# Moving small VectorE steps between the groups of a fused attention and gated feed-forward kernel

## The chip, the cores and the metric

The kernel runs on one core of a Trainium2 chip. A core has five engines that run their own streams of instructions and wait for each other by semaphores: PE (TensorE, matmuls), DVE (VectorE), ACT (ScalarE), POOL (GpSimd) and SP (SyncE, which here only issues DMAs). The metric is the device time of one execution in microseconds (us); less is better.

## What is computed

The reference, cut to its core: a linear attention without softmax, an RMS norm per head, and a gated feed-forward layer over all tokens.

```python
# q, k, v: (8 batches, 8 heads, 576 tokens, 64)
kv  = einsum('bhsd,bhse->bhde', k, v)
out = einsum('bhsd,bhde->bhse', q, kv)
x   = out / sqrt(mean(out * out, axis=-1) + 1e-6) * g_norm   # then (4608, 512)
g, val = x @ w_gate, x @ w_val                               # (4608, 1536)
gelu = 0.5 * g * (1 + erf(g / sqrt(2)))
ffn_out = gelu * val @ w_out
result = x + sigmoid(x @ w_res) * ffn_out
```

## The kernel before

**Blocks.** Each of the 8 batches gives a block of 512 tokens, as four rows of tiles (j = 0 to 3, 128 tokens by 512 columns). The 64 tokens of each batch that are left over, the "last tokens", are gathered two batches to a row into a ninth block, number 8. The attention of batch b is worked out while TensorE does the feed-forward of blocks b-2 and b-1: `a_o` multiplies q by kv, `a_sq` and `a_red` make the sums of squares `ss`, `a_norm` makes the reciprocal roots `ny` (on POOL from batch 2 on), `a_t` scales the attention's output by them into the tile `t` (L341, VectorE), `a_x` multiplies a row of `t` by g in place (L355, VectorE), and `d_xT` transposes rows of `t` into `xT` with a DMA on SP's queue. For batches 4 to 7 `a_t(b, 4)` scales the last tokens; its source is not a PSUM bank but the SBUF tile `o32`, one of three buffers that it shares with the tiles `c` named below.

**A block's two stages.** In the first, the gate and value products, TensorE multiplies `xT` by `w_gate` and `w_val`. For the last third of block 0 and from the fifth column tile of block 2 on, this is done in groups of four column tiles (`gv_group`), with seven products in place of eight, of sums of weights and of tokens (`ts`). Block 2 has two such groups, blocks 3 to 8 have three. Each group is a list of words, written out by hand; for groups that are not the last of a block it reads

```python
"1g 1v Eg 5g Ev 5v dg 6g dv 6v Fg 2g Fv 2v 7g g11 7v cg 3g cv 3v h11 g12 4g g21 h12 4v g22 h21 h22"
```

A number is a product on TensorE (four matmuls, L736) for the gate (g) or the value (v): 1, 4, 6, 7 add to a PSUM bank A, 2 to E, 3 and 5 to F. E and d are copies on ScalarE (bank A to E, L746; F to the SBUF tile d, L750). F and c are sums on VectorE (L757): F puts A + d back into bank F, c puts A + d into an SBUF tile `c`. g11 to g22 are gelus on ScalarE (L767), h11 to h21 products with the value on VectorE, and h22 the same on POOL (L773). A product that adds to a bank waits until those who read the bank before are done: 6 for E, 7 for F, 4 for c.

In the second stage (`out_by_products`) come the residual gate (`m_res`), then seven products with `w_out` in banks named wA to wF, `s_rest` (VectorE sums of hidden tiles), the multiplication with the gate `pf` (L527), the addition of `t` on POOL (`fin`, L531), and `store`, a DMA on SP's queue. The calls of `aside` put VectorE and POOL steps of the coming block between the products. For block 1 alone (`later`) the steps `a_x`, `fin` and `store` are put into block 2's groups, since its `t` is multiplied by g only then.

**What sets the order.** Every engine executes its instructions in the order in which this program issues them. `at_word(block, i, word, *steps)` issues steps directly behind a word in the i-th group of a block; `at` and `aside_out` do so behind a slot and inside the second stage. The steps that are moved:

- block 1's rows in block 2: `a_x(1, 0..3)` (x0 to x3), four `fin`, two `store`; L570 to L573;
- in blocks 3 to 6 (`whole(m + 1)`), for the batch that follows, b = 4 to 7: `a_t(b, 2)` to `a_t(b, 4)` (t2, t3, t4), `a_x(b, 0..4)` (x0 to x4), two `d_xT`; L1220 to L1231.

At the end of block 2's last group stands `load_behind` (L1134), with which POOL issues the loads of the next batch; behind it POOL does `a_norm`.

Of the kernel before, what the change touches and what calls it, by code (L numbers as in the profile page):

```python
# [18 lines left out]
def kernel(  # L19
# [22 lines left out]
    NJ = 4  # L42
# [284 lines left out]
    def where(b, j):  # L327
        return (b, j) if j < NJ else (B, pair(b))
# [40 lines left out]
    def d_xT(b, j0, j1):  # L369
        blk, k0 = where(b, j0)  # L370
        k1 = k0 + j1 - j0
        nc.sync.dma_start(
            out=xT_t[blk][:, k0:k1, :, :].rearrange("p j c t -> p (j c) t"),
            in_=t_t[blk][:, k0:k1, :].rearrange("p j c -> p (j c)"),
            transpose=True,
        )
# [35 lines left out]
    def m_res(blk, j, bank):  # L412
        rps = pmoe.tile([P, C], FP32, name="rps", bank=bank)
        for cc in range(NP):
            nc.tensor.matmul(  # L415
                rps,
                lhsT=xT_t[blk][:, j, cc, :],
                rhs=wr16[:, cc, :],
                start=(cc == 0),
                stop=(cc == NP - 1),  # L420
            )

        th = th_all[:, j, :]
        nc.scalar.activation(out=th, in_=rps, func=AF.Tanh, scale=0.5)  # L424
        return th
# [30 lines left out]
    def b_of(i, j):  # L456
        return wo16[:, (i - 1) * NFH : i * NFH, (j - 1) * CH : j * CH]

    def a_of(blk, i, j):
        return hids[blk][:, (j - 1) * NFH : j * NFH, (i - 1) * PR : i * PR]  # L460
# [20 lines left out]
    def s_last(blk):  # L481
        sub(nc.vector, hid_sums[3], a_of(blk, 1, 2), hid_sums[1])
# [14 lines left out]
    def out_by_products(blk, later, banks, amid):  # L497
        w = {}
        s_ = hid_sums

        def aside(ahead_of):
            for f in amid.get(ahead_of, ()):
                f()

        def res(jj):
            for j in (2 * jj, 2 * jj + 1):
                m_res(blk, j, banks[j])

        def first_two():
            for n in ("D", "E", "F", "A"):  # L510
                w[n] = pmoe.tile([P, 2, CH], FP32, name="w" + n, bank=banks[n])
            w["d"] = attnp.tile([P, 2, CH], FP32, tag="sq", bufs=3, name="wd")
            s_last(blk)
            prod(w["A"], a_of(blk, 1, 1), b_of(1, 1), True)
            nc.scalar.copy(out=w["E"], in_=w["A"])
            aside("D")
            prod(w["D"], s_[0], wo_t[:, 0], True)
            nc.scalar.copy(out=w["d"], in_=w["D"])
            aside("gates")
            for j in range(NJ):  # L520
                m_sigmoid(j)

        def part(jj):
            return slice(None), slice(2 * jj[0], 2 * jj[0] + 2), slice(jj[1] * CH, (jj[1] + 1) * CH)

        def pf(jj, src, eng=nc.vector):
            eng.tensor_tensor(out=res_all[part(jj)], in0=th_all[part(jj)], in1=src, op=ALU.mult)  # L527

        def fin(jj):
            of = part(jj)  # L530
            nc.gpsimd.tensor_tensor(out=res_all[of], in0=res_all[of], in1=t_t[blk][of], op=ALU.add)  # L531

        def store(jj):
            dst = out[blk * S : blk * S + M0, :].rearrange("(p j) c -> p j c", j=NJ)
            js = slice(2 * jj, 2 * jj + 2)
            nc.sync.dma_start(out=dst[:, js, :], in_=res_all[:, js, :])

        def others():


            prod(w["A"], s_[1], wo_t[:, 1], False)
            aside("F")
            sub(nc.vector, w["F"], w["A"], w["d"], ALU.add)
            aside("00")
            prod(w["E"], a_of(blk, 1, 2), b_of(2, 1), False)
            pf((0, 0), w["E"])
            aside("22")
            prod(w["A"], s_[2], wo_t[:, 2], False)
            c22 = res_all[part((1, 1))]
            sub(nc.vector, c22, w["A"], w["d"], ALU.add)  # L550
            aside("01")
            prod(w["F"], s_[3], b_of(2, 2), False)
            pf((0, 1), w["F"])
            aside("11")
            prod(w["A"], a_of(blk, 2, 2), wo_t[:, 3], False)
            if whole(blk + 1):
                pf((1, 1), c22, nc.gpsimd)
                pf((1, 0), w["A"])
            else:
                pf((1, 1), c22)  # L560
                pf((1, 0), w["A"])
            if later:
                return
            for i in (1, 0):
                fin((i, i))
                fin((i, 1 - i))
                store(i)

        if later:
            x = [lambda j=j: a_x(blk, j) for j in range(NJ)]  # L570
            at_word(blk + 1, 0, "Fv", x[0])
            at_word(blk + 1, 0, "h21", *x[1:3], lambda: fin((0, 0)), lambda: fin((0, 1)), lambda: store(0))
            at_word(blk + 1, 1, "Fv", x[3], lambda: fin((1, 0)), lambda: fin((1, 1)), lambda: store(1))  # L573
        return [lambda: res(0), lambda: res(1), first_two, others]

    def out_last(blk, banks):
# [243 lines left out]
    for which in "kv":  # L820
        if which == "k":
            t = hidp.tile([P, NF, NJ * P], FP16, tag="hid", name=which + "f").rearrange("p a b -> p (a b)")
        else:
            t = hid_s
# [8 lines left out]
    for which in "kv":  # L833
        t = hid_of[which]
# [336 lines left out]
    def at_word(blk, i, word, *fs):  # L1171
        amid_gv.setdefault((blk, i), {}).setdefault(word, []).extend(fs)
# [5 lines left out]
    def plan_attn_ahead(b):  # L1178

        rem = pair(b) is not None  # L1180
        m = b - 2
        assert rem == (m in GROUPS)
        act, pool = nc.scalar.copy, nc.gpsimd
        begin = [lambda: attn_begin(b), lambda: d_qT(b)]
        if rem:
            begin.append(lambda: d_rem_qT(b))
        if m in GROUPS:
            for i in range(2):
                half = lambda i=i: by_token(b, act, slice(2 * i, 2 * i + 2))
                if whole(m):  # L1190
                    at_word(m, i, "g11", half)
                else:
                    at(m, 2 + i, half)
            if whole(m):
                at_word(m, 1, "g11", *begin)
            else:
                at(m, 3, *begin)
            if b + 1 < B:
                at(m, 2 * GF, lambda: load_behind(b))
            last = len(GROUPS[m]) - 1  # L1200
        else:
            at(m, 8, lambda: by_token(b, act, slice(0, 2)))
            at(m, 9, lambda: by_token(b, act, slice(2, 4)), *begin)
            at(m, NF - 1, lambda: a_kv(b, act))
            at(m, NF, lambda: load_behind(b))
        if rem:
            own = 2 * pair(b) + 1 == b
            at_word(m, last, "5v" if own else "3v", lambda: a_rem_kv(b))
            at_word(m, last, "dv" if own else "g12", lambda: kv_out(b))
            at_word(m, last, "h21", *[lambda: rem_mm(b)] * own, lambda: rem_out(b), lambda: a_sq(b, NJ))  # L1210
        at(m, NF, lambda: a_o(b), *[lambda: a_red(b, NJ)] * rem, lambda: a_ss(b, 0), lambda: a_ss(b, 1))
        aside_out(m, "D", lambda: a_ss(b, 2), lambda: a_ss(b, 3))
        aside_out(m, "F", lambda: a_norm(b, 0, NJ + rem, pool))
        first = [lambda: new_block(b), lambda: a_t(b, 0), lambda: a_t(b, 1)]
        if whole(m + 1):
            aside_out(m, "11", *first)
        else:
            at(m, NF + 3, *first)
        if whole(m + 1):
            t = [lambda j=j: a_t(b, j) for j in range(NJ + 1)]  # L1220
            x = [lambda j=j: a_x(b, j) for j in range(NJ + 1)]
            for i, word, fs in (
                (0, "Fv", t[2:3]),
                (0, "cv", t[3:4]),
                (0, "h21", t[4:5]),
                (1, "1v", x[0:1]),
                (1, "Fv", x[1:2]),
                (1, "cv", x[2:3]),
                (2, "1v", [x[3], lambda: d_xT(b, 0, NJ), x[4], lambda: d_xT(b, NJ, NJ + 1)]),
            ):  # L1230
                at_word(m + 1, i, word, *fs)  # L1231
            return
        for j in range(2, NJ + rem):
            at(m + 1, j - 2, lambda j=j: a_t(b, j))
        for j in range(NJ):
            at(m + 1, 2 + j // 2, lambda j=j: a_x(b, j))
        at(m + 1, 3, lambda: d_xT(b, 0, NJ))
        if rem:
            at_word(m + 1, 0, "h21", lambda: a_x(b, NJ), lambda: d_xT(b, NJ, NJ + 1))
# [13 lines left out]
    for blk in GROUPS:  # L1253
        t = token_sums(blk, nc.vector)
# [160 lines left out]
```

## Time and profile before

| | |
|---|---|
| median of 4 runs | 325.11 us (324.84 to 326.05) |
| the profiled execution | 325.38 us, of which the span from first to last instruction 323.5 us |
| granted TensorE clock, mean | 0.995 |
| PE busy | 315.7 us, 98% of the span |
| DVE busy | 264.7 us, 82% |
| ACT busy | 201.5 us, 62% |
| POOL busy | 145.9 us, 45% |

All are of one profiled execution but the first. A busy share is time with at least one instruction in work; PE's matmuls are pipelined and their ends are modelled, so that a PE that is busy all the time may still have its steps start late.

The stages that the change touches, in us from the span's start, with the busy time in each:

| stretch | stage | PE | DVE | ACT | POOL |
|---|---|---|---|---|---|
| 98.1 to 104.2 | block 2, first group | 6.10 | 5.22 | 4.25 | 0.00 |
| 104.2 to 111.4 | block 2, last group | 7.20 | 6.51 | 5.16 | 5.66 |
| 111.4 to 124.7 | block 2, second stage | 13.30 | 11.77 | 8.81 | 12.25 |
| 124.7 to 131.2 | block 3, first group | 6.43 | 5.31 | 4.52 | 5.58 |
| 131.2 to 137.6 | block 3, second group | 6.40 | 6.40 | 5.25 | 1.16 |
| 137.6 to 144.9 | block 3, third group | 7.30 | 7.11 | 5.13 | 2.88 |

Blocks 4 to 6 repeat block 3's pattern every 33.2 us.

### The profile page before, as it was taken

The page shows a single profiled execution, that of the slowest core. Times are in us where ns is not written, and L with a number is a line of the kernel's source. Part 1 is how long each engine was busy: PE and PEld are TensorE (multiplying, and loading weights), DVE is VectorE, ACT ScalarE, POOL GpSimd, SP SyncE. Part 2 cuts the span into 40 slices and gives each one's busy share as a digit, 9 for nine tenths or more (in the row PEclk, how much of TensorE's full clock was granted, in tenths as well). Part 3 has the DMA queues.
Part 4 walks back from the last instruction along what each step waited for, and adds up shares of the span by engine and source line. Part 5 has one row for each costly group of instructions (what it writes and reads, how often), then busy time and mean ns, then how long its engine had stood idle before and what let it go on. Part 6 is the DMA issues. An engine that isn't in the chain of part 4 may idle for free.

```text
span 323.5 us, 7457 instructions
## 1 busy us (share of the span) xinstructions
PE 315.7 (98%) x2936; PEld 236.9 (73%) x2936; DVE 264.7 (82%) x482; ACT 201.5 (62%) x367; POOL 145.9 (45%) x212
## 2 busy tenths in 40 slices
PE   8999999999999999999999999999999999999993
PEld 3544755445858778887888688868887888788782
DVE  5788879799798897998799879898996777677754
ACT  3673685365737783778486848684766467636760
POOL 2792351573700999247833784117511242042232
PEclk9999999999999999999999999999999999999998
DMA  7999999799995489299938893820321030002004
GB/s 252 325 203 204 194 205 180 167 178 136 153 138 107 141 134 146 114 161 131 98 132 164 110 120 131 127 41 2 130 50 33 2 130 4 0 30 104 0 2 130
DMA packets 76693, 38.89 MB, mean 120 GB/s; under 512 B 42098, under 2 KB 74354, under 8 KB 76658
## 3 DMA queue, kind: packets, MB, share of 16 engines
q0 software_dynamic: 38752, 17.17, 42.4%
q1 hardware_dynamic: 37328, 20.71, 24.6%
q8 instruction: 23, 0.38, 0.5%
q10 hardware_dynamic: 578, 0.52, 0.5%
q14 instruction: 12, 0.10, 0.1%
HBM read 38.80 MB, written 9.44 MB: 149 GB/s over the span
## 4 chain that ended last, share of the span: by engine, by line
PE 96%; DVE 3%; ACT 0%; issue 0%; DVEq 0%; ACTq 0%
PE Av L736 12%; PE Ag L736 11%; PE wA L488 11%; PE rps L415 10%; PE gps L395 6%; PE vps L395 6%; PE Fg L736 6%; PE Fv L736 6%; PE fps L432 3%; PE Ev L736 3%; PE Eg L736 3%; PE wE L488 3%; PE wD L488 3%; PE wF L488 3%; PE w L488 2%; PE idle L901 2%
## 5 line engine op out<-in xcount | busy, mean ns | idle before, releaser
L773 POOL TENSOR_TENSOR hid<-ge,c 128x512 f16<-128x512 f16 x21 | 25.4, 1207 | 65.0 <-ACT ge L767 65.0
L531 POOL TENSOR_TENSOR osb<-osb,t 128x512 f32<-128x512 f32 x28 | 31.7, 1164 | 41.3 <-DVE osb L527 25.2
L488 PEld LDWEIGHTS <-hid_s 128*128 128x128 f16 x384 | 37.6, 98 | 4.3
L736 PEld LDWEIGHTS <-wsv 128*128 128x128 f16 x336 | 32.8, 98 | 5.1 <-issue 0.9
L736 PEld LDWEIGHTS <-wsg 128*128 128x128 f16 x336 | 32.7, 98 | 4.4
L415 PE MATMUL rps<-wr,xT 128*128 128x512 f16 x144 | 33.4, 380 | 0.0
L488 PEld LDWEIGHTS <-hid 128*128 128x128 f16 x288 | 28.2, 98 | 5.0
L746 ACT COPY Eg<-Ag 128x512 f32<-128x512 f32 x21 | 12.2, 583 | 25.9 <-PE Ag L736 25.9
L757 DVE TENSOR_TENSOR Fg<-Ag,d 128x512 f32<-128x512 f32 x21 | 14.6, 695 | 15.8 <-ACT d L750 10.9
L383 ACT ACTIVATE ge<-gps 128x512 f16<-128x512 f32 x24 | 14.1, 597 | 21.3 <-PE gps L395 21.1
L736 PEld LDWEIGHTS <-wg 128*128 128x128 f16 x252 | 24.4, 98 | 3.3
L736 PEld LDWEIGHTS <-wv 128*128 128x128 f16 x252 | 24.6, 98 | 3.0
L424 ACT ACTIVATE th<-rps 128x512 f32<-128x512 f32 x36 | 21.1, 595 | 8.0 <-PE rps L415 8.0
L736 PE MATMUL Av<-ts,wsv 128*128 128x256 f16 x168 | 25.2, 272 | 0.1
L736 PE MATMUL Ag<-ts,wsg 128*128 128x256 f16 x168 | 25.2, 272 | 0.0
L254 DVE TENSOR_REDUCE ss<-sq 128x8 f32<-128x512 f32 x32 | 20.1, 678 | 4.7 <-ACT sq L249 4.6
L415 PEld LDWEIGHTS <-xT 128*128 128x128 f16 x144 | 13.5, 98 | 14.2
L395 PE MATMUL gps<-xT,wg 128*128 128x512 f16 x88 | 22.6, 379 | 0.0
L395 PE MATMUL vps<-xT,wv 128*128 128x512 f16 x88 | 22.6, 379 | 0.0
L488 PE MATMUL wA<-wo_ts,hid_s 128*128 128x256 f16 x168 | 20.6, 273 | 0.0
L384 DVE TENSOR_TENSOR hid<-ge,vps 128x512 f16<-128x512 f16 x24 | 16.3, 684 | 4.8 <-PE vps L395 4.0
L429 ACT ACTIVATE th<-th 128x512 f32<-128x512 f32 x36 | 20.1, 642 | 0.0
(188 smaller groups left out, 766.8 us busy)
## 6 DMA issues: line engine op xcount, KB each, us to landing
out_dram<-osb SPq DMA_DIRECT2D x14, 512.0 KB, 2.6
qraw<-in_q_dram POOLq DMA_DIRECT2D x7, 512.0 KB, 6.9
k<-in_k_dram POOLq DMA_DIRECT2D x7, 512.0 KB, 9.6
v<-in_v_dram POOLq DMA_DIRECT2D x7, 512.0 KB, 11.6
wg<-in_moe_w_gate_dram POOLq DMA_DIRECT2D x2, 512.0 KB, 8.2
wv<-in_moe_w_val_dram POOLq DMA_DIRECT2D x2, 512.0 KB, 8.9
wo<-in_moe_w_out_dram POOLq DMA_DIRECT2D x2, 512.0 KB, 13.6
out_dram<-osb SPq DMA_DIRECT2D x4, 256.0 KB, 4.5
```

Of the source, the lines that this page charges most:

```text
L254: nc.vector.tensor_reduce(out=out_, in_=sqs.pop((b, i)), op=ALU.add, axis=mybir.AxisListType.X)
L383: nc.scalar.activation(out=ge, in_=gps, func=AF.Gelu)
L384: nc.vector.tensor_tensor(out=hids[blk][:, f, :], in0=ge, in1=vps, op=ALU.mult)
L395: nc.tensor.matmul(ps[:, j0 * P : j1 * P], lhsT=w[:, cc, :], rhs=xT_t[blk][:, j0:j1, cc, :], start=(cc == 0 and j0 == 0), stop=(cc == NP - ...
L415: nc.tensor.matmul(rps, lhsT=xT_t[blk][:, j, cc, :], rhs=wr16[:, cc, :], start=(cc == 0), stop=(cc == NP - 1),)
L424: nc.scalar.activation(out=th, in_=rps, func=AF.Tanh, scale=0.5)
L429: nc.scalar.activation(out=th, in_=th, func=AF.Copy, scale=0.5, bias=0.5)
L488: nc.tensor.matmul(ps[:, e - es[0], :], lhsT=a[:, f, e * P : (e + 1) * P], rhs=b[:, f, :], start=(start and e == es[0] and f == 0), stop=( ...
L531: nc.gpsimd.tensor_tensor(out=res_all[of], in0=res_all[of], in1=t_t[blk][of], op=ALU.add)
L736: nc.tensor.matmul(out_[:, r, :], lhsT=lhsT, rhs=rhs, start=(first and r == 0 and c == 0), stop=(c == 1), skip_group_check=True,)
L757: nc.vector.tensor_tensor(out=dst, in0=ps["A", u], in1=sb["d", u], op=ALU.add)
L773: eng.tensor_tensor(out=dst, in0=ge[q], in1=source(q, "v"), op=ALU.mult)
```

## The change

It moves steps between words and leaves all arithmetic as it is.

```diff
@@ out_by_products, block 1's rows in block 2
             x = [lambda j=j: a_x(blk, j) for j in range(NJ)]
-            at_word(blk + 1, 0, "Fv", x[0])
-            at_word(blk + 1, 0, "h21", *x[1:3], lambda: fin((0, 0)), lambda: fin((0, 1)), lambda: store(0))
-            at_word(blk + 1, 1, "Fv", x[3], lambda: fin((1, 0)), lambda: fin((1, 1)), lambda: store(1))
+            at_word(blk + 1, 0, "1v", *x[0:2], lambda: fin((0, 0)), lambda: fin((0, 1)), lambda: store(0))
+            at_word(blk + 1, 0, "Fv", x[2])
+            at_word(blk + 1, 0, "cv", x[3])
+            at_word(blk + 1, 0, "h22", lambda: fin((1, 0)), lambda: fin((1, 1)), lambda: store(1))
@@ plan_attn_ahead, batches 4 to 7 in blocks 3 to 6
                 (0, "Fv", t[2:3]),
                 (0, "cv", t[3:4]),
-                (0, "h21", t[4:5]),
                 (1, "1v", x[0:1]),
-                (1, "Fv", x[1:2]),
-                (1, "cv", x[2:3]),
-                (2, "1v", [x[3], lambda: d_xT(b, 0, NJ), x[4], lambda: d_xT(b, NJ, NJ + 1)]),
+                (1, "Fv", t[4:5]),
+                (1, "cv", x[1:2]),
+                (2, "1v", [*x[2:4], lambda: d_xT(b, 0, NJ)]),
+                (2, "Fv", [x[4], lambda: d_xT(b, NJ, NJ + 1)]),
```

So t4 goes from the end of the first group into the second, behind Fv; x1 goes from Fv to cv of the second group, x2 from there into the third, x4 from the third group's start behind its Fv. In block 2 all four products with g and all four `fin` are issued in the first group, two of each at its start.

## The prediction

> **What bounds the kernel now.** I read the page's chain of waits first: it is TensorE nearly alone.
>
> ```profile
> PE 96%; DVE 3%; ACT 0%; issue 0%; DVEq 0%; ACTq 0%
> ```
>
> So only what makes TensorE stand still counts, and a busy share hides that, since matmuls overlap. I therefore read the timeline of TensorE by the starts of its steps. In a group (L736) a step is four matmuls, and undisturbed steps start 0.437 us apart; a longer distance is a stall. I took all distances from block 2 to the end. Block 2 has none over 0.44, blocks 7 and 8 none either. In blocks 3 to 6 the second group always has two. Block 3:
>
> ```profile
> 133.84 0.60 PE L736 MATMUL Eg<-xT,wg 128*128 128x256 f16 x4
> 134.28 0.60 PE L736 MATMUL Ev<-xT,wv 128*128 128x256 f16 x4
> 134.85 0.60 PE L736 MATMUL Ag<-ts,wsg 128*128 128x256 f16 x4
> 135.44 0.60 PE L736 MATMUL Av<-ts,wsv 128*128 128x256 f16 x4
> 135.88 0.60 PE L736 MATMUL Fg<-xT,wsg 128*128 128x256 f16 x4
> ```
>
> The columns are start, duration, engine. 134.28 to 134.85 is 0.57 (0.13 lost), 134.85 to 135.44 is 0.59 (0.155 lost). In blocks 4, 5, 6 the same two lose 0.29, 0.285, 0.295. These are words 7g and 7v: they add to bank A, so they wait until VectorE has read A in Fg and Fv. VectorE there:
>
> ```profile
> 133.04 0.81 DVE L341 TENSOR_TENSOR t<-o,ny 128x512 f16<-128x512 f32 x1
> 133.77 0.41 DVE L355 TENSOR_TENSOR t<-t,g 128x512 f16<-128x512 f16 x1
> 134.11 0.69 DVE L757 TENSOR_TENSOR Fg<-Ag,d 128x512 f32<-128x512 f32 x1
> 134.71 0.68 DVE L757 TENSOR_TENSOR Fv<-Av,d 128x512 f32<-128x512 f32 x1
> 135.31 0.41 DVE L355 TENSOR_TENSOR t<-t,g 128x512 f16<-128x512 f16 x1
> 135.64 0.68 DVE L757 TENSOR_TENSOR c<-Ag,d 128x512 f32<-128x512 f32 x1
> 136.24 0.68 DVE L757 TENSOR_TENSOR c<-Av,d 128x512 f32<-128x512 f32 x1
> ```
>
> Fg ends at 134.79 and 7g starts 0.06 later; Fv ends at 135.39, 7v starts 0.05 later. In front of Fg stand the scaling of the last tokens (t4, 0.73 to the next start) and a product with g (0.34). The copies d that Fg and Fv need end on ScalarE at 133.69 and 134.17, so they are not the bound.
>
> **Edit 1, t4 from h21 of the first group to Fv of the second (blocks 3 to 6).** The product x0 now starts at 133.04. A POOL product (hid, L773) runs until 133.30; a product with g that meets one is held to its end and ends 0.28 later:
>
> ```profile
> 138.58 1.16 POOL L773 TENSOR_TENSOR hid<-ge,c 128x512 f16<-128x512 f16 x1 [5.28 <-ACT ge L767]
> 138.96 1.06 DVE L355 TENSOR_TENSOR t<-t,g 128x512 f16<-128x512 f16 x1
> ```
>
> So x0 ends at 133.59, before d: free. Fg then starts with d, at 133.75 (VectorE starts 0.03 to 0.09 after a ScalarE copy), ends 134.44; Fv 134.35 to 135.03. Undisturbed, 7g is due at 134.72 and 7v at 135.16: both stalls go. What is late next: t4 (0.68 without POOL beside it, like t2; step 0.60) runs 134.95 to 135.63, cg 135.55 to 136.24, cv 136.15 to 136.83. 4g (due 136.47) is free; 4v (due 136.90) needs cv plus 0.055, so within 0.02. The first group, which has t2 at the same word, loses 0.04 there. I take 0.03 lost against 0.29 gained. Bounds for t4: 0.60 as t2, or 0.73 as it was; with 0.73 cv ends 0.13 later and 4v loses 0.12. It had the POOL product until 133.30 beside it, so I take 0.60. cg also now writes the o32 buffer that t4 has just read; a step that must wait for its predecessor on VectorE (the second ts of L463) starts 0.03 after its end instead of 0.08 before, so at worst 0.11 more.
>
> **Edit 2, the products spread.** The second group has x0, x1 instead of x0, x1, x2; the third has x2, x3 ahead of Fg as x3, x4 were, then x4 at Fv. x2 is held by the POOL product as x3 was, but this product hangs on 4g through ScalarE (g21, g22) and moves forward with TensorE. The third group's one stall (0.06 at 7v in three blocks) keeps or absorbs the 0.03. x4 at Fv costs 0.34 in front of cg, which idled 0.19 for TensorE: cg 0.05 to 0.15 late, and in the last group's order 4g comes after 3g, 3v and (in three blocks) 1.1 us of small matmuls: nothing. SP's transposes: x0 to x3's is issued when two products are through, as now (140.11; SP was busy with qrT before it); the one row of x4 follows it in the queue anyway, and both must be in by the next block's first ts sum at 153.9. Nothing.
> Net of both edits: 4 x 0.28 = **-1.12**.
>
> **Edit 3, block 1's rows sooner in block 2.** Nothing stalls in block 2, so nothing is to be had in it. Behind it there is: in block 3's first group 6v starts 0.23 late.
>
> ```profile
> 124.27 0.27 POOL L315 TENSOR_TENSOR ny<-nh,ny 128x40 f32<-128x40 f32 x1
> 124.58 1.29 DVE L341 TENSOR_TENSOR t<-op,ny 128x512 f16<-128x512 f32 x2 [0.25 <-POOL ny L315]
> 125.78 0.68 DVE L527 TENSOR_TENSOR osb<-th,wA 128x512 f32<-128x512 f32 x1
> 126.55 0.57 ACT L746 COPY Ev<-Av 128x512 f32<-128x512 f32 x1 [0.59 <-DVE osb L527]
> 127.17 0.60 PE L736 MATMUL Av<-ts,wsv 128*128 128x256 f16 x4
> ```
>
> POOL's norm ends late, so t, so pf, so the seed Ev. The norm starts at 120.03, straight behind POOL's loads (to 119.96), though its last ss was there at 119.53. The loads start late since four fins (1.16 each) stand in the way of POOL's two products in block 2, the second of which ends at 113.51. With the fins ahead, it ends near 111.5, the loads near 118.1, and the norm starts with ss, 0.4 sooner. Block 4, where POOL is free, loses 0.06 in its first group against 0.355 in block 3: **-0.30**. The earlier loads lie beside VectorE's s_rest. Beside such sums (0.95 each) the loads' issues last 0.98 and 0.89 as elsewhere, so neither loses by it; the slack is 119.6 against 118.1, and if more than that were lost, the -0.30 would shrink to nothing.
>
> The price is in block 2's first group. x0 and x1 go to VectorE at 99.66, into the 0.82 that it idles before Fg (100.57), and end at 100.41: free. fin starts 0.08 after x1, at 100.49 (now 105.74, x1's end 105.66), and the second runs from 101.61 to 102.77. x2 comes behind Fv at 101.77, in the middle of it. Now:
>
> ```profile
> 101.77 0.41 DVE L355 TENSOR_TENSOR t<-t,g 128x512 f16<-128x512 f16 x1
> 102.25 0.69 DVE L757 TENSOR_TENSOR c<-Ag,d 128x512 f32<-128x512 f32 x1
> 107.89 0.53 DVE L355 TENSOR_TENSOR t<-t,g 128x512 f16<-128x512 f16 x1
> ```
>
> The last row is a product beside fins and lost only 0.11; by it x2 ends at 102.30, cg starts on time, and the price is nothing. [...] x2 would wait 1.00: end 103.06, cg 102.98 to 103.67, cv to 104.27; 4g (due 103.35) starts at 103.73, 4v (then due 104.17) at 104.33: 0.38 + 0.16 = **+0.54**. [...] The ends are 0 and 0.54. x3 after cv meets an idle POOL. [...] Stores stand in SP's queue behind qT and qrT (to 105.96) as before.
>
> **Sum.** -1.12 - 0.30 + 0.54 = -0.88: span 323.50 to 322.6. The profiled execution took 325.38 (1.88 around its span), 0.27 over the median 325.11; I subtract from the median: **324.2 us**. A measurement of this kernel can tell about 0.3% (0.98) from no change; the forecast lies just inside.
>
> **The rivals.**
> - **The second fin starts late, x2 slips in front of it** (or the row of 0.11 is right): -1.42, 323.7. For: only 0.16 lies between fin's start and x2's. Against: the waits of POOL on VectorE are 0.08 to 0.10 throughout.
> - **The stall moves to 4v**: t4 at 0.73 or the buffer's turn costs 0.11 to 0.13 in each second group: gain 0.18 x 4 = 0.72; -0.72 - 0.30 + 0.54 = -0.48, 324.6.
> - **Slower**: t4 in front of cg takes both, 0.73 and the buffer wait. cg then ends at 136.48, cv at 137.08: 4g loses 0.07, 4v 0.16 more, and with g22 and POOL's product later the third group loses the rest: no gain in four blocks. With +0.54 and the norm no earlier (POOL's slack of 1.5 used up by slower loads): 325.65; it decides from about 0.25 in front of 4v on. For more than 0.3%, another 0.1 per group is needed.
> - That the order doesn't change as written: nothing in the trace speaks for it.
>
> **How the numbers follow.** Forecast 0.47 (half of it beyond -0.3%, as -0.88 lies at 0.98's edge), slip 0.22 (faster), moved stall 0.16 (same), slower 0.15 (0.10 of it over 0.3%). Faster 0.42, same 0.47, slower 0.11. Range: from full gains (-1.6, 323.5) to the zero of the groups (325.4).
>
> **What would show it.** In blocks 3 to 6 the second group's 7g and 7v at 0.44, 4v at most 0.50. In block 3's first group 6v at 0.44 and the norm starting with ss. In block 2's first group x2 near 1.3 us and steps of about 0.8 and 0.6 at 4g and 4v. Wrong if x2 lasts 0.4, if t4 lasts 0.8 with POOL idle, or if a stall appears in the third groups.

## The result and the profile after

The changed kernel takes 324.59 us (median of 34 runs; 325.05 for 56 runs of the kernel before beside them). The ratio is 0.9985, 95% interval 0.9979 to 0.9991: about 0.49 us less, clear of zero and within 0.3%. The profiled execution took 324.50 us with a span of 322.7.

The chain of waits of the changed kernel, as shown of before:

```profile
PE 93%; DVE 2%; DMA 2%; SPq 1%; POOL 0%; issue 0%; DVEq 0%
```

It is still TensorE; the new DMA share lies in the opening (the first 12 us; one load, of `kf`, makes 5.47 of them, from 4.31 on), before any step that was moved. The opening differs between executions: block 2 starts at 90.73 to 91.58 us in the nine profiles of this study, whose programs are the same up to there but for one copy. So I compare stages by their lengths, from a block's first gate product to the next block's; where two kernels do the same in a block, the lengths agree within 0.02 us.

| block | 2 | 3 | 4 | 5 | 6 | sum |
|---|---|---|---|---|---|---|
| before | 33.54 | 33.46 | 33.16 | 33.20 | 31.37 | 164.73 |
| after | 34.04 | 33.05 | 32.86 | 33.15 | 31.08 | 164.18 |
| difference | +0.50 | -0.41 | -0.30 | -0.05 | -0.29 | -0.55 |

Block 7 takes 30.96 in both. Blocks 4 and 6 gained what was forecast; block 2 lost what was forecast; block 5 gained next to nothing, and block 3 less than it should have. TensorE's timeline in block 3's second group of the changed kernel (start, duration, engine; the rows are the words 6g, 6v, 2g, 2v, 7g, 7v):

```profile
132.93 0.60 PE L737 MATMUL Ag<-ts,wsg 128*128 128x256 f16 x4
133.48 0.60 PE L737 MATMUL Av<-ts,wsv 128*128 128x256 f16 x4
133.91 0.60 PE L737 MATMUL Eg<-xT,wg 128*128 128x256 f16 x4
134.35 0.60 PE L737 MATMUL Ev<-xT,wv 128*128 128x256 f16 x4
134.78 0.60 PE L737 MATMUL Ag<-ts,wsg 128*128 128x256 f16 x4
135.31 0.60 PE L737 MATMUL Av<-ts,wsv 128*128 128x256 f16 x4
```

7g is on time, but 6v comes 0.55 behind 6g (0.11 lost), and 7v 0.53 behind 7g (0.09 lost). With 0.05 at 4v this is 0.25, against 0.29 before: the stall has a new place. 6v adds to bank A, which Ev reads on ScalarE:

```profile
131.92 0.59 ACT L747 COPY Eg<-Ag 128x512 f32<-128x512 f32 x1
132.86 0.57 ACT L747 COPY Ev<-Av 128x512 f32<-128x512 f32 x1 [0.34 <-PE Fg L737]
133.34 0.59 ACT L751 COPY d<-Fg 128x512 f32<-128x512 f32 x1
133.82 0.60 ACT L751 COPY d<-Fv 128x512 f32<-128x512 f32 x1
```

In the kernel before:

```profile
131.96 0.59 ACT L746 COPY Eg<-Ag 128x512 f32<-128x512 f32 x1
132.62 0.57 ACT L746 COPY Ev<-Av 128x512 f32<-128x512 f32 x1
```

Ev starts 0.34 after Eg's end, where it started 0.06 after it before. That makes d late, and with d Fg and Fv on VectorE:

```profile
133.00 0.54 DVE L355 TENSOR_TENSOR t<-t,g 128x512 f16<-128x512 f16 x1
133.96 0.70 DVE L758 TENSOR_TENSOR Fg<-Ag,d 128x512 f32<-128x512 f32 x1 [0.42 <-ACT d L751]
134.57 0.69 DVE L758 TENSOR_TENSOR Fv<-Av,d 128x512 f32<-128x512 f32 x1
135.17 0.68 DVE L341 TENSOR_TENSOR t<-o,ny 128x512 f16<-128x512 f32 x1
135.77 0.68 DVE L758 TENSOR_TENSOR c<-Ag,d 128x512 f32<-128x512 f32 x1
```

VectorE now idles 0.42 in front of Fg. The profile names TensorE's 5g as what Ev waited for. But Ev doesn't read F, the bank that 5g writes, and in block 4, which is the same code, Ev starts on time, before its 5g (165.11, 0.60 long by the profile's modelled end) is through:

```profile
164.98 0.59 ACT L747 COPY Eg<-Ag 128x512 f32<-128x512 f32 x1
165.63 0.57 ACT L747 COPY Ev<-Av 128x512 f32<-128x512 f32 x1
```

In blocks 3 and 5 Ev is late, in 4 and 6 it is not. I counted ScalarE's instructions in the two traces, waits on semaphores included, from 0 on. Ev of block 3 is number 191, Ev of block 5 number 319, exactly 128 further on. Before, both were number 190 and 318, and the numbers 191 and 319 were the copy d, which queues behind the running Ev anyhow. The changed kernel has one ScalarE instruction more (522, not 521): in block 2's last group a gelu now waits for POOL as well as for TensorE, and one of the two waits became an instruction of its own (number 149, where the gelu itself was before). So theory A: a place in ScalarE's stream that comes every 128 instructions costs about 0.28 us (0.34 against 0.06), and the change moved it onto an instruction that TensorE waits for. Theory B: the edits themselves make Ev late.

### The profile page after: what moved, and what is told of

It is laid out like the page before. It is cut to its first block, busy times and chain, and to the rows that moved or that the text cites. A ratio compares the mean times of both kernels' runs of the same rounds, so it can differ in the third digit from the quotient of the medians.

```text
span 322.7 us, 7458 instructions
## 1 busy us (share of the span) xinstructions
PE 314.7 (98%) x2936; PEld 236.4 (73%) x2936; DVE 264.0 (82%) x482; ACT 201.5 (62%) x367; POOL 145.0 (45%) x212
## 4 chain that ended last, share of the span: by engine, by line
PE 93%; DVE 2%; DMA 2%; SPq 1%; POOL 0%; issue 0%; DVEq 0%
PE Av L737 12%; PE Ag L737 12%; PE wA L488 11%; PE rps L415 10%; PE gps L395 6%; PE vps L395 6%; PE Fv L737 6%; PE Fg L737 6%; PE fps L432 3%; PE wF L488 3%; PE wE L488 3%; PE wD L488 3%; PE Eg L737 3%; PE Ev L737 3%; PE w L488 2%; DMA kf<-in_k_dram 2%
## 5 line engine op out<-in xcount | busy, mean ns | idle before, releaser
L774 POOL TENSOR_TENSOR hid<-ge,c 128x512 f16<-128x512 f16 x21 | 24.5, 1165 | 68.5 <-ACT ge L768 68.5
```

Of the source, the lines that this page charges most:

```text
L774: eng.tensor_tensor(out=dst, in0=ge[q], in1=source(q, "v"), op=ALU.mult)
```

## The experiments

**Edits 1 and 2 alone, and edit 3 alone.** The first takes the kernel after with L570 to L573 of the kernel before, the second the reverse.

```diff
-            at_word(blk + 1, 0, "1v", *x[0:2], lambda: fin((0, 0)), lambda: fin((0, 1)), lambda: store(0))
-            at_word(blk + 1, 0, "Fv", x[2])
-            at_word(blk + 1, 0, "cv", x[3])
-            at_word(blk + 1, 0, "h22", lambda: fin((1, 0)), lambda: fin((1, 1)), lambda: store(1))
+            at_word(blk + 1, 0, "Fv", x[0])
+            at_word(blk + 1, 0, "h21", *x[1:3], lambda: fin((0, 0)), lambda: fin((0, 1)), lambda: store(0))
+            at_word(blk + 1, 1, "Fv", x[3], lambda: fin((1, 0)), lambda: fin((1, 1)), lambda: store(1))
```

> Edits 1 and 2 alone (t4 and the products with g in blocks 3 to 6), block 1's rows as before. Theory A (ScalarE's stream): in the changed kernel the seed Ev of blocks 3 and 5 starts 0.28 us late because a place in ScalarE's own instruction stream, one instruction further on than before, falls on it; the extra instruction is a wait that edit 3 put into block 2. Without edit 3 the stream is as before, so all four second groups lose at most 0.05 each instead of 0.29, block 2 has no stall, block 3's first group keeps its 0.355: 1.1 us under before, 323.95. Theory B (the edits themselves make Ev late in blocks 3 and 5): those two second groups lose about 0.25 as in the changed kernel: 0.6 under before, 324.4.

> Edit 3 alone (block 1's rows sooner in block 2), t4 and the products of blocks 3 to 6 as before. Block 2's first group loses 0.34 at 4g and 0.16 at 4v, block 3's first group gains 0.30. By theory A Ev starts 0.28 late in blocks 3 and 5, but there t4 and x0 still hold back 7g and 7v, which hides it: second groups lose 0.29 as before. Sum 0.2 us over before: 325.25. Theory B: Ev is on time in blocks 3 and 5; the time is the same, so that Ev's start in the trace decides, not the time.

Edits 1 and 2 alone: 323.94 us, ratio to before 0.9959 (0.9944 to 0.9974); blocks 33.54, 33.18, 32.87, 32.91, 31.07, sum -1.16. ScalarE has 521 instructions again, and in the second groups of blocks 3 to 6 no step is longer than 0.44. Theory A's numbers. Block 3's first group keeps its 0.37.

Edit 3 alone: 325.15 us, ratio 0.9994 (0.9982 to 1.0006), which doesn't tell +0.2 from nothing; by blocks 34.04, 33.15, 33.15, 33.19, 31.36, sum +0.16: +0.50 in block 2, -0.31 in block 3. It has 522 instructions on ScalarE, and Ev is late in block 3 although nothing in blocks 3 to 6 was edited. Its ScalarE timeline:

```profile
131.71 0.59 ACT L747 COPY Eg<-Ag 128x512 f32<-128x512 f32 x1
132.64 0.57 ACT L747 COPY Ev<-Av 128x512 f32<-128x512 f32 x1 [0.34 <-PE Fg L737]
```

6v loses 0.11 there, 7g 0.02 and 7v 0.16: again 0.29, as t4 and x0 hold Fg back for as long. Theory B falls.

**One more ScalarE copy.** The kernel after, with a copy of one element into a tile that nothing reads, in block 1:

```diff
+    spare = consts.tile([1, 1], FP16, name="spare")
...
                 slots[s]()
+                if blk == 1 and s == 1:
+                    for _ in range(1):
+                        nc.scalar.copy(out=spare, in_=g16[0:1, 0:1])
```

> The changed kernel with one more ScalarE instruction in block 1, a copy of one element that nobody waits for. Theory A: ScalarE's stream moves on by one, the place falls on the wait in front of Ev while Eg still runs, and Ev of blocks 3 and 5 starts on time: their second groups lose 0.05 instead of 0.25, 0.4 us under the changed kernel, 324.15. Theory B: nothing changes, 324.6.

323.95 us, ratio 0.9960 (0.9944 to 0.9976); blocks 34.05, 32.86, 32.87, 32.91, 31.08, sum -0.96. An instruction more made it 0.41 us shorter over these blocks. Numbers 191 and 319 are now the semaphore waits in front of Ev, and Ev is on time:

```profile
132.30 0.59 ACT L747 COPY Eg<-Ag 128x512 f32<-128x512 f32 x1
132.95 0.57 ACT L747 COPY Ev<-Av 128x512 f32<-128x512 f32 x1
133.44 0.59 ACT L751 COPY d<-Fg 128x512 f32<-128x512 f32 x1
```

The place should then come a third time, 128 behind 319. With the copy, number 447 is a gelu in block 7's last group, where no step was moved and the two kernels run the same code. It starts 0.76 after ScalarE's instruction before it, where in the changed kernel (there it is number 446) it starts 0.49 after it. The first row is from the kernel with the copy, the second from the changed one:

```profile
270.95 0.60 ACT L768 ACTIVATE ge<-Eg 128x512 f16<-128x512 f32 x1 [0.76 <-PE Eg L737]
270.73 0.60 ACT L768 ACTIVATE ge<-Eg 128x512 f16<-128x512 f32 x1 [0.49 <-PE Eg L737]
```

From the start of block 7, this gelu comes 0.28 later in the two kernels with 523 instructions than in all seven others. No step of TensorE waits for it, and block 7 takes 30.96 in all nine.

**The same copy in the kernel before.**

> The kernel before with the one more ScalarE copy in block 1 and nothing else. Theory A: Ev of the second groups of blocks 3 and 5 starts 0.28 later than it did, 6v loses 0.11 there, and 7g loses that much less, since t4 and x0 hold VectorE's Fg back anyway: stalls of 0.29 in sum and blocks 3 to 6 as long as before, so that the place in the stream costs nothing here: 325.05. Theory B: Ev on time.

324.95 us, ratio 0.9998 (0.9988 to 1.0009); blocks 33.54, 33.45, 33.15, 33.19, 31.36. Ev is late in blocks 3 and 5 (6v loses 0.11), and no block is longer: 7g loses 0.02 instead of 0.13, 7v 0.16 as it did. The place was dear only once edit 1 had taken away the later stall that hid it.

**The fins later.** The other loss, block 2's +0.50. In the kernel after, the timelines of VectorE and then of POOL show x2 (101.55) and the two fins:

```profile
101.55 1.27 DVE L355 TENSOR_TENSOR t<-t,g 128x512 f16<-128x512 f16 x1
102.74 0.68 DVE L758 TENSOR_TENSOR c<-Ag,d 128x512 f32<-128x512 f32 x1
103.34 0.68 DVE L758 TENSOR_TENSOR c<-Av,d 128x512 f32<-128x512 f32 x1
103.94 0.41 DVE L355 TENSOR_TENSOR t<-t,g 128x512 f16<-128x512 f16 x1
```

```profile
100.26 2.27 POOL L531 TENSOR_TENSOR osb<-osb,t 128x512 f32<-128x512 f32 x2 [10.59 <-DVE t L355]
```

The fins end at 102.53, x2 0.28 later. TensorE's 4g waits for the c that comes behind x2:

```profile
102.69 0.60 PE L737 MATMUL Fv<-xT,wsv 128*128 128x256 f16 x4
103.47 0.60 PE L737 MATMUL Ag<-ts,wg 128*128 128x256 f16 x4 [0.18 <-DVE c L758]
104.06 0.60 PE L737 MATMUL Av<-ts,wv 128*128 128x256 f16 x4
```

4g comes 0.78 behind 3v, 4v 0.60 behind 4g: 0.34 and 0.16. To take POOL's work from beside x2, and nothing else:

```diff
-            at_word(blk + 1, 0, "1v", *x[0:2], lambda: fin((0, 0)), lambda: fin((0, 1)), lambda: store(0))
+            at_word(blk + 1, 0, "1v", *x[0:2])
...
+            at_word(blk + 1, 0, "h22", lambda: fin((0, 0)), lambda: fin((0, 1)), lambda: store(0))
             at_word(blk + 1, 0, "h22", lambda: fin((1, 0)), lambda: fin((1, 1)), lambda: store(1))
```

> The changed kernel with the first two fin of block 1's rows issued behind h22 too, in front of the other two, so that POOL is idle while x2 runs. If x2 is held by the fin beside it: x2 takes 0.41 instead of 1.27, block 2's first group loses nothing instead of 0.50, the norm behind block 2 still starts with ss, 0.5 us under the changed kernel, 324.1. If the position of x2 in front of cg is to blame and not POOL: x2 0.41 but cg late and 4g still waits, 0.1 to 0.3 lost, 324.3 to 324.5.

324.19 us, ratio 0.9960 (0.9943 to 0.9977); blocks 33.54, 33.05, 32.86, 33.13, 31.07, sum -1.08. In block 2 x2, in the same position, takes 0.42 and no step waits:

```profile
101.30 0.42 DVE L355 TENSOR_TENSOR t<-t,g 128x512 f16<-128x512 f16 x1
101.77 0.69 DVE L759 TENSOR_TENSOR c<-Ag,d 128x512 f32<-128x512 f32 x1
```

So the price was POOL's, not the position's. Blocks 3 and 5 keep their 0.25.

**Three products at once.** The fins stay early, x2 goes in front of them:

```diff
-            at_word(blk + 1, 0, "1v", *x[0:2], lambda: fin((0, 0)), lambda: fin((0, 1)), lambda: store(0))
-            at_word(blk + 1, 0, "Fv", x[2])
+            at_word(blk + 1, 0, "1v", *x[0:3], lambda: fin((0, 0)), lambda: fin((0, 1)), lambda: store(0))
```

> The changed kernel with x2 moved from Fv to 1v in block 2, behind x0 and x1, where VectorE idles; the fins stay at 1v. If x2 is lost to the fin beside it alone: x2 runs before the first fin's turn ends or meets it at its start, Fg starts at about 0.1 later than now and block 2's first group loses at most 0.05 instead of 0.50: 0.45 under the changed kernel. If three products are too many for that idle time: Fg and Fv late, 7g and 7v lose 0.1 to 0.3. Blocks 3 and 5 keep their 0.25 (ScalarE's stream as in the changed kernel).

324.08 us, ratio 0.9972 (0.9964 to 0.9979); blocks 33.54, 33.06, 32.86, 33.15, 31.07, sum -1.05. Fg starts 0.10 later in the block than in the kernel after, and that costs nothing.

**Both losses mended:** three products, and the one more copy.

> The kernel of the run before with the one more ScalarE copy in block 1: both losses gone. Blocks 2 to 6 together 1.45 us shorter than before's, if the two losses are independent; 323.6. If they share a cause, 0.5 to 0.9 shorter.

324.03 us as a median of only 7 runs between 323.28 and 324.53, ratio 0.9963 (0.9949 to 0.9977); blocks 33.54, 32.86, 32.85, 32.91, 31.07, sum -1.50, as forecast for independent losses. The interval lies below that of the changed kernel, each taken against the kernel before in its own round, so this version is faster than both. The 323.6 was not met by the median; against edits 1 and 2 alone the times don't decide, only the lengths do (163.23 against 163.57).

## Why the prediction was right, and where it was wrong

The time (324.2 forecast, 324.59 measured) lies in the range, and "within 0.3%" was called the likeliest class. Of the forecast gain of 0.88, some 0.5 came. That the class came true is in part luck. My own weights give 0.455 for faster (half of 0.47, and 0.22) and 0.445 for the same (the other half, 0.16 and 0.05), not 0.42 and 0.47. And the gain stayed within 0.3% because of a loss that I had not forecast: with one copy more on ScalarE, which takes that loss away, the blocks gain 0.96 and the ratio is 0.9960.

- **+0.54 in block 2: right, 0.50.** That x2 would stand until the second fin's end was my estimate, and no run shows the 0.54 itself. In its place the runs showed this: x2 started 0.17 behind the second fin, ended 0.28 after it and took 1.27, where with the fins moved it took 0.42; 4g and 4v lost 0.34 and 0.16. In the kernel before, the held product of 1.06 and the three like it in blocks 4 to 6 end 0.28 after their POOL product too. The row of 0.11 was cheap since it met a fin 0.24 before that fin's end; it, too, ended 0.28 after it. The rival in which x2 slips through fell, since the fin was first. A product that was first did slip through: in the kernel before, x1 and x2 (the first row) took 0.42 each; x2 starts at 105.58, 0.16 ahead of the fin, and ends at 106.00, beside it.

```profile
105.24 0.75 DVE L355 TENSOR_TENSOR t<-t,g 128x512 f16<-128x512 f16 x2
105.74 2.39 POOL L531 TENSOR_TENSOR osb<-osb,t 128x512 f32<-128x512 f32 x2 [15.83 <-PE Fg L736]
```

- **-0.30 in block 3's first group: right, -0.31.** POOL's second product ended at 111.24 (111.5 forecast), the loads at 118.14 (118.1), and the norm followed its ss. It started 5.13 before block 3's first product, where it had started 4.72 before it: 0.41 sooner, as forecast.

```profile
119.89 0.22 POOL L302 TENSOR_SCALAR nm<-ss 128x40 f32<-128x40 f32 x1 [1.76 <-DVE ss L254]
```

- **-1.12 in the groups: wrong size, -0.73.** Blocks 4 and 6 gave 0.30 and 0.29 (0.28 forecast); blocks 3 and 5 gave 0.04 each in the second group, block 3 some 0.05 more in the third. The step that failed is "Fg then starts with d, at 133.75": I took the copies d to end where they had ended, since they were not edited. They ended at 133.93, because Ev came 0.28 late. By themselves edits 1 and 2 gave -1.16, so their own sum was right. What it lacked is that edit 3 adds a wait to ScalarE's stream, and that the stall which edit 1 removes would have covered a late Ev, as it does in the kernel before with the copy. I had asked what was late next behind Fg, on VectorE, and took everything in front of it, on ScalarE, as given.
- **t4 at 0.60 and no turn of the buffer: right.** t4 took 0.68, and cg started 0.08 before its end, so it waits for nothing. The 0.81 before stood beside a POOL product that ran until 133.30; in the changed kernel POOL is idle beside t4. 4v loses 0.05. The rival in which the stall moves to 4v, and the slower one built on it, fell.
- **x0 held beside POOL's product: right**, it ended at 133.54 (133.59 forecast), 0.28 after that product, and was free. x4 at Fv of the third group and the transposes cost nothing: no third group loses more than before.

That the place is tied to a number in ScalarE's stream and can cost 0.28 is shown by the kernels above: Ev is late with 522 instructions on ScalarE, on time with 521 and 523, and with 523 the gelu at 447 is late. The period of 128 rests on these three places. That it is the fetching of instructions is my guess: no run changed the fetches. What speaks for it is where they lie. The profile counts them as a queue of their own (q14 instruction, 12 packets, 0.10 MB), and in all nine traces one of 8 KB starts 0.06 to 0.75 us behind the starts of numbers 191, 319 and 447; behind each late Ev of the changed kernel it is 0.65. The delay didn't show where the instruction was held up anyway: number 191 of the kernel before, the copy d, started 0.48 behind an Ev of 0.57, as it does in block 4 of the changed kernel, where Ev is on time. What sets the place within the stream was not tried.

## What to carry to other kernels

Before counting a removed stall as a gain, look at every other input of the waiting instruction, also on an engine that nobody edited, and ask whether the change can delay it: a moved step can add a wait to another engine's stream, as it did here (522 instructions on ScalarE, not 521), and the stall that is removed no longer covers such a delay (0.28 here). When a step is moved onto VectorE beside a POOL step, look in the trace for which of them starts first: here a product with g took 1.27 when it started 0.17 behind a fin, and 0.42 when it started 0.16 ahead of one. In this kernel it paid to put the short VectorE products in front of the fins that they feed (block 2 at 33.54 in place of 34.04). Compare block lengths, not times, when effects are below the scatter of the opening, and when identical code is late in every second block, count the instructions of the late engine.

## What the runs showed that I had not expected

A semaphore wait more in block 2 moved a delay of 0.28 us, which stands at numbers 191 and 319 of ScalarE's stream, onto the copies Ev of blocks 3 and 5, 21 and 87 us later, and so cost 0.4 us; a useless copy of one element brought it back. In the kernel before, the same shift cost nothing.
